# Layer 1's weights made slice by slice in one double slot, with cast and subtraction over 1024 columns

## The chip, the core and the metric

One core of a Trainium2 chip runs the whole program. The metric is the device time of one execution in microseconds, as the median of several executions. A profiled execution also gives its span, from the first to the last instruction of the program. TensorE is called PE here, VectorE DVE, ScalarE ACT and SyncE (which issues the transfers) SP, as in the profile.

## The reference

The program computes an attention layer with a memory term and sends its output through two dense layers.

```python
def _attn_ref(q, k, v, M_prev, z_prev, beta):          # B, H, S, D = 4, 8, 576, 64
    scores = scale * np.matmul(q, k.transpose(0, 1, 3, 2))     # causal mask, softmax -> a
    local = np.matmul(a, v)
    mem_out = mem_ret / mem_norm                       # phi(q) @ M_prev over phi(q) . z_prev
    return g * mem_out + (1 - g) * local

def _moe_ref(x, w_in, w_out, s, b):                    # x: 2304 x 512, w_in: 512 x 2048
    r = np.maximum(x @ w_in, 0.0)
    return (s * (r * r) + b) @ w_out

def _moe2_ref(x, w_in, w_out, alpha):
    h = x @ w_in
    return (np.maximum(h, 0.0) + alpha * np.minimum(h, 0.0)) @ w_out

def reference(**kwargs):
    x = rows of attn_out                               # 2304 x 512
    return _moe2_ref(x=_moe_ref(x=x, **moe), **moe2)
```

The weights of both layers arrive as 64-bit floats, so each number is two 32-bit words in memory.

## The kernel before

**Layers.** The hidden size 2048 of a dense layer is cut into 16 slices of 128 (`KF`, index `f`). For a block of tokens `g1` multiplies x with slice f of `w_in` (12 matmuls, L923 to L925), ACT and DVE make the activation (L937, L938, L945 on ACT, L946 on DVE), and `g2` multiplies it with slice f of `w_out` (12 matmuls, L964 to L966). Every float32 operand is split in a high and a low part, and three matmuls replace one: high times high, high times low, low times high. Layer 1 works on one block of 512 tokens (block 0) and then on blocks of 256; layer 2 on blocks of 512.

**Weights.** `weights` prepares one slice. For each of the two matrices a transfer (L859, 512 KB) brings 128 x 512 numbers as 128 x 1024 words into a double slot `st`. Three DVE instructions over 512 columns (L862, L865, L868) put the float32 bits together from the two words in a slot `sw`. ACT copies them to the high part of `wt` (L871), and DVE subtracts the high part from the number, which gives the low part (L874). Layer 1's weights stay in SBUF. They are made while block 0 runs, so block 0 is the place where slices are used for the first time. `w_in` of a slice is made first, and `g1` needs nothing of `w_out`.

**Attention** goes in four batches. Batch 0 has to be finished up to token 512 before block 0 can start. Batch 1 is computed beside block 0, batches 2 and 3 beside the blocks of 256. Its DVE lines are, among others, L740 (the largest score of a row), L605 (low part of the softmax weights), L482 (low part of the values), L526 to L530 (memory term); its PE lines L520, L565, L655, L671 and L767.

**Order.** `Plan` collects all operations with a duration and a priority, and `order` walks through them as a list scheduler: at each step the engine that is free first takes the operation with the best priority whose inputs are there and for which slots can be had. The outcome is a fixed order for each engine. `Slot` objects get their places in `spot`: 19 slots (`pool`, `poolx`), and early in the run also 12 places in the four `room` tiles, three to a tile, where the weights of the last four slices will stand later. A change of one operation's duration, slot or inputs can so reorder all engines until the two plans meet again.

Of the kernel before, what the change touches and what calls it, by code (L numbers as in the profile page):

```python
# [6 lines left out]
F32 = mybir.dt.float32  # L7
# [3 lines left out]
I32 = mybir.dt.int32  # L11
# [15 lines left out]
NP = H // 2  # L27
# [13 lines left out]
NSLOT = 19  # L41

XS = 7
RES = dict(fq=7, fe=3, fa=1, k=5, v=5, vf=3, p=2, w=1, xt=0, st=6, st2=4, wb=3, wb2=1, x=0)
W1GATE = 1
YS = 4
XF = 4
# [31 lines left out]
class Plan:  # L79
# [17 lines left out]
    def op(self, eng, dur, fn, r=(), w=(), prio=None, bytes_=0, claim=()):  # L97
        i = len(self.ops)
        deps, late = set(), set()
        for k in r:  # L100
            if k in self.writer:
                deps.add(self.writer[k])
            self.readers.setdefault(k, []).append(i)
        for k in w:
            if k in self.writer:
                deps.add(self.writer[k])
            late.update(self.readers.get(k, ()))
            self.writer[k] = i
            self.readers[k] = []
        late -= deps  # L110
        late.discard(i)
        deps.discard(i)
        slots = []
        for k in list(r) + list(w):
            s = k[0] if isinstance(k, tuple) else k
            if isinstance(s, Slot) and s not in slots:
                slots.append(s)
                s.left += 1
        self.ops.append((eng, dur, fn, deps | late, i + self.lean if prio is None else prio, bytes_, slots, late, claim))
        return i  # L120
# [8 lines left out]
    def order(self):  # L129
# [29 lines left out]
        def is_free(x, t):  # L159
            return x not in closed and x not in closing and not taken[x] and place_free[x] <= t  # L160

        def spot(t, s):

            if isinstance(s, Bank):
                return min((x for x in (self.nslots + self.nextra + y for y in s.banks) if is_free(x, t)),
                           key=lambda x: place_free[x], default=None)
            if s.early:
                for x in reversed(places[self.nslots + s.above:self.nslots + self.nextra]):
                    if is_free(x, t) and (s.size == 1 or (x - self.nslots) % 3 < 2 and is_free(x + 1, t)):
                        return x  # L170
            base = [x for x in places[:self.nslots] if is_free(x, t)]
            if len(base) < s.reserve + s.size:
                return None
            if s.size == 2:
                base = [x for x in base if x + 1 in base and x + 1 != self.edge]
            return min(base, key=lambda x: place_free[x], default=None)

        def take(t, new):
# [123 lines left out]
def t_dve(n, rate=1.04, extra=0.0):  # L302
    return 69 + n * rate + extra


def t_act(n, fixed=93.0, extra=0.0):
    return fixed + n * 0.834 + extra


def build(tc, kp, vd, qp, mzd, beta8, sb2, win1, wout1, win2, wout2, alpha, outT):  # L310
# [8 lines left out]
    with tc.tile_pool(name="sb", bufs=1) as sb, tc.tile_pool(  # L319
# [9 lines left out]
        def wt(f, x, lo):  # L329
            if f not in made:  # L330
                made[f] = sb.tile([128, 4, DM], F32R, name=f"wt{f}", tag=f"wt{f}")
            return made[f][:, 2 * x + lo, :]
# [43 lines left out]
        def at(s, n, dt=F32):  # L376

            if s.place < NSLOT:
                t, j = (pool, s.place) if s.place < NSLOT - XS else (poolx, s.place - NSLOT + XS)
                v = t[:, j * GW:(j + s.size) * GW]  # L380
            else:
                f, j = divmod(s.place - NSLOT, 3)
                v = room[KF - XF + f][:, j * GW:(j + s.size) * GW]
            return (v if dt == F32 else v.bitcast(dt))[:, 0:n]
# [445 lines left out]

        def weights(win, wout, f, layer):
            prio = None
            if layer == 1:
                prio = marks[int(WP)] + (WP - int(WP)) * (marks[1] - marks[0])
            claim = []
            if layer == 1 and f >= KF - XF:
                claim = [NSLOT + 3 * (f - KF + XF) + j for j in range(3)]
            above = max(0, 3 * (f + 1 - KF + XF))  # L840
            for src, x, key in ((win, 0, "wi"), (wout, 1, "wo")):
                sw = Slot(RES["wb" if layer == 1 else "wb2"], layer == 1, above=above)

                def whole(sw=sw, dt=F32):
                    return at(sw, 512, dt)

                st = Slot(RES["st" if layer == 1 else "st2"], layer == 1, 2, above)

                def word(x, st=st):
                    return at(st, 1024, I32).rearrange("p (n t) -> p n t", t=2)[:, :, x]  # L850

                gate = []

                first = layer == 2 and f == x == 0
                if layer == 2:
                    gate = [("x1", B - 1, NP - 1, 1)] if first else ["claimed"]
                elif W1GATE:
                    gate = [("x1", 0, min(NP - 1, f // W1GATE), 1)]
                op("SP", 475, lambda st=st, src=src: nc.sync.dma_start(  # L859
                    out=at(st, 1024, I32), in_=src[f]), r=gate, w=[st] + (["claimed"] if first else []), prio=prio, bytes_=524288,  # L860
                   claim=list(range(NSLOT - XS, NSLOT)) if first else [])
                op("DVE", t_dve(512, 0.52), lambda word=word, whole=whole: V.tensor_scalar(  # L862
                    out=whole(dt=I32), in0=word(1), scalar1=3, scalar2=0x3FFFFFF8, op0=ALU.logical_shift_left,
                    op1=ALU.bitwise_and), r=[st], w=[sw], prio=prio)
                op("DVE", t_dve(512), lambda word=word, whole=whole: V.scalar_tensor_tensor(  # L865
                    out=whole(dt=I32), in0=word(0), scalar=29, in1=whole(dt=I32), op0=ALU.logical_shift_right,
                    op1=ALU.bitwise_or), r=[st], w=[sw], prio=prio)
                op("DVE", t_dve(512), lambda word=word, whole=whole: V.scalar_tensor_tensor(  # L868
                    out=whole(dt=I32), in0=word(1), scalar=-0x40000000, in1=whole(dt=I32), op0=ALU.bitwise_and,
                    op1=ALU.bitwise_or), r=[st], w=[sw], prio=prio)  # L870
                either("w", t_act(512), lambda whole=whole, x=x: A.copy(out=wt(f, x, 0), in_=whole()),  # L871
                       t_dve(512, 0.52), lambda whole=whole, x=x: V.tensor_copy(out=wt(f, x, 0), in_=whole()),
                       r=[sw], w=[(key, "h", f)], prio=prio, claim=claim)
                op("DVE", t_dve(512), lambda whole=whole, x=x: V.tensor_tensor(  # L874
                    out=wt(f, x, 1), in0=whole(), in1=wt(f, x, 0).bitcast(F32), op=ALU.subtract),
                   r=[sw, (key, "h", f)], w=[(key, "l", f)], prio=prio)
# [267 lines left out]
```

## Time and profile before

| what | before |
|---|---|
| median of 3 executions | 994.93 us (994.38 to 996.17) |
| the profiled execution, own time | 995.49 us |
| its span | 993.5 us |
| PE busy | 976.9 us, 98% |
| DVE busy | 603.6 us, 61% |
| ACT busy | 469.8 us, 47% |
| granted TensorE clock, mean | 1.000 of full speed |

The busy shares are means over stages with very different limits, and the end of a matmul is modelled in the profile, so a PE that reads as busy throughout is not necessarily issuing at its full rate. The stage of the weights of layer 1 lies between about 28 us and 172 us.

### The profile page before, as it was taken

How to read it: one execution, taken by the hardware profiler on the slowest of the kernel's cores; microseconds unless marked ns; L12 is line 12 of the kernel's file. 1: busy time of each engine (PE TensorE's matmuls, PEld its weight loads, DVE VectorE, ACT ScalarE, POOL GpSimd, SP SyncE). 2: the span in 40 equal slices, each digit the busy share in tenths (PEclk: the TensorE clock that was granted, in tenths of full speed). 3: DMA queues.
4: the chain of work that ended last, by engine and by line, in shares of the span. 5: the costliest groups of instructions: out<-in, count | busy, mean ns of one | idle time of the engine just before them, and what ended most of it. 6: DMA issues, size and time to landing. Idle time of an engine off the chain costs nothing.

```text
span 993.5 us, 18027 instructions
## 1 busy us (share of the span) xinstructions
PE 976.9 (98%) x7068; PEld 833.1 (84%) x7068; DVE 603.6 (61%) x1473; ACT 469.8 (47%) x1181; POOL 5.6 (1%) x29
## 2 busy tenths in 40 slices
PE   7999999999999999999999999999999999999998
PEld 5777777788888888999999998888888888888898
DVE  7999998677776767432122999945334443534354
ACT  7877766787777777545445653212112110201111
POOL 1000000000000000000000000000000000000000
PEclk9999999999999999999999999999999999999999
DMA  5359955464667565721000655302000200100010
GB/s 174 99 171 237 233 187 156 103 164 111 149 131 150 146 127 106 179 77 44 1 22 22 215 168 183 125 1 85 1 1 11 64 1 1 43 1 0 1 44 22
DMA packets 114693, 93.23 MB, mean 94 GB/s; under 512 B 83376, under 2 KB 94640, under 8 KB 114608
## 3 DMA queue, kind: packets, MB, share of 16 engines
q1 hardware_dynamic: 114608, 92.08, 34.3%
q8 instruction: 55, 0.90, 0.4%
q14 instruction: 30, 0.25, 0.1%
HBM read 59.29 MB, written 13.11 MB: 73 GB/s over the span
## 4 chain that ended last, share of the span: by engine, by line
PE 90%; DVE 4%; ACT 3%; DMA 1%; issue 1%; SPq 0%; ACTq 0%; DVEq 0%
PE yb L964 14%; PE yb L966 13%; PE yb L965 13%; PE hb L923 9%; PE hb L925 8%; PE hb L924 8%; PE sp L924 3%; PE sp L925 3%; PE sp L923 3%; PE ob L767 2%; PE ob L924 2%; PE ob L923 2%; PE ob L925 2%; PE yb L767 2%; PE sp L671 2%; PE sp L767 2%
## 5 line engine op out<-in xcount | busy, mean ns | idle before, releaser
L964 PE MATMUL yb<-gr,wt 128*128 128x256 f32 (+2 forms) x832 | 273.1, 328 | 0.7 <-ACT gr L945 0.5
L966 PE MATMUL yb<-gr,wt 128*128 128x256 f32 (+2 forms) x832 | 271.3, 326 | 0.0
L965 PE MATMUL yb<-gr,wt 128*128 128x256 f32 (+2 forms) x832 | 270.0, 324 | 0.0
L923 PE MATMUL hb<-xr,wt 128*128 128x256 f32 (+1 forms) x592 | 184.5, 312 | 5.0 <-ACT gt L937 3.5
L925 PE MATMUL hb<-xr,wt 128*128 128x256 f32 (+1 forms) x592 | 180.2, 304 | 0.3 <-DVE wt L874 0.3
L924 PE MATMUL hb<-xr,wt 128*128 128x256 f32 (+1 forms) x592 | 180.0, 304 | 0.0
L964 PEld LDWEIGHTS yb<-gr,wt 128*128 128x128 f32 x832 | 157.0, 189 | 19.3 <-issue 3.1
L966 PEld LDWEIGHTS yb<-gr,wt 128*128 128x128 f32 x832 | 156.8, 188 | 15.3 <-DVE gr L946 1.1
L965 PEld LDWEIGHTS yb<-gr,wt 128*128 128x128 f32 x832 | 156.9, 189 | 13.8
L946 DVE TENSOR_TENSOR gr<-gt,gr 128x256 fp32r<-128x256 f32 (+1 forms) x168 | 84.0, 500 | 135.9 <-ACT gr L945 135.0
L945 ACT CAST gr<-gt 128x256 fp32r<-128x256 f32 (+1 forms) x168 | 78.4, 467 | 147.8 <-DVE gt L943 140.2
L923 PEld LDWEIGHTS hb<-xr,wt 128*128 128x128 f32 x592 | 111.7, 189 | 18.2 <-ACT gt L937 5.5
L925 PEld LDWEIGHTS hb<-xr,wt 128*128 128x128 f32 x592 | 111.6, 189 | 6.3 <-DVE wt L874 0.7
L924 PEld LDWEIGHTS hb<-xr,wt 128*128 128x128 f32 x592 | 111.7, 189 | 5.0
L937 ACT ACTIVATE gt<-hb 128x256 f32<-128x256 f32 (+1 forms) x128 | 52.5, 410 | 99.9 <-PE hb L925 98.0
L945 ACT CAST gr<-mz 128x512 fp32r<-128x512 f32 (+1 forms) x40 | 23.1, 578 | 157.6 <-DVE mz L943 157.5
L925 PE MATMUL sp<-xr,wt 128*128 128x512 f32 (+1 forms) x160 | 59.4, 371 | 0.0
L924 PE MATMUL sp<-xr,wt 128*128 128x512 f32 (+1 forms) x160 | 59.3, 371 | 0.0
L923 PE MATMUL sp<-xr,wt 128*128 128x512 f32 (+1 forms) x160 | 59.2, 370 | 0.0
L938 ACT ACTIVATE gt<-gt 128x256 f32<-128x256 f32 (+1 forms) x128 | 56.9, 444 | 2.6
L946 DVE TENSOR_TENSOR gr<-mz,gr 128x512 fp32r<-128x512 f32 (+1 forms) x40 | 25.5, 638 | 25.0 <-ACT gr L945 25.0
L940 DVE TENSOR_SCALAR mz<-ob,alv 128x512 f32<-128x512 f32 (+1 forms) x20 | 13.9, 697 | 39.6 <-PE ob L925 39.6
(349 smaller groups left out, 1488.4 us busy)
## 6 DMA issues: line engine op xcount, KB each, us to landing
pool<-wout SPq DMA_DIRECT2D x18, 512.0 KB, 4.4
pool<-win SPq DMA_DIRECT2D x16, 512.0 KB, 4.0
room<-wout SPq DMA_DIRECT2D x14, 512.0 KB, 3.8
room<-win SPq DMA_DIRECT2D x13, 512.0 KB, 4.2
pool<-y SPq DMA_DIRECT2D x18, 256.0 KB, 3.3
out_t<-pool SPq DMA_DIRECT2D x16, 256.0 KB, 2.4
pool<-x SPq DMA_DIRECT2D x11, 256.0 KB, 3.1
y<-pool SPq DMA_DIRECT2D x21, 128.0 KB, 1.8
```

The lines of the kernel that those rows point to most:

```text
L671: T.matmul(obk[D * odd:D * odd + D, AT[c] - o0:AT[c] - o0 + nq], W[:, kb, odd, w], p_t(k)[:, y:y + nq], start=False, stop=False, skip_grou ...
L767: T.matmul(bank_at(bk)[rows, x:x + n], half(sqp, odd, q0, nq), half(sk, odd, k0, n), start=True, stop=True, skip_group_check=True)
L923: T.matmul(H_, W_h, X_h, start=(d == 0), stop=False)
L924: T.matmul(H_, W_h, X_l, start=False, stop=False)
L925: T.matmul(H_, W_l, X_h, start=False, stop=(d == KD - 1))
L937: op("ACT", t_act(n, 50), lambda: A.activation(out=t_, in_=H_, func=AF.Relu), r=[hk, "gr"], w=[tk], prio=-1)
L938: op("ACT", t_act(n), lambda: A.activation(out=t_, in_=t_, func=AF.Square), w=[tk], prio=-1)
L945: op("ACT", t_act(n), lambda: A.copy(out=G_h, in_=t_), r=[tk], w=[("gh", gj)], prio=-1)
L946: op("DVE", t_dve(n), lambda: V.tensor_tensor(out=G_l, in0=t_, in1=G_h.bitcast(F32), op=ALU.subtract), r=[tk, ("gh", gj)], w=[("gl", gj)], ...
L964: T.matmul(Y, W_h, G_h, start=first, stop=False, skip_group_check=True)
L965: T.matmul(Y, W_l, G_h, start=False, stop=False, skip_group_check=True)
L966: T.matmul(Y, W_h, G_l, start=False, stop=False, skip_group_check=True)
```

## The change

Layer 1 gets a function of its own, `both`. It takes one slot `sw` of size two for both matrices of a slice, with the words of `w_in` in the left 512 columns and those of `w_out` in the right 512. The three DVE instructions that build the bits stay as they are, 512 columns each, once for each matrix. The copy on ACT and the subtraction on DVE then go once over 1024 columns, written as two halves because the high and low parts of the two matrices alternate in `wt`. Both wait for the words of both matrices. The reserve of these slots goes from 3 to 2, and `spot` can place slots of any size. Layer 2 keeps its code.

```diff
-RES = dict(fq=7, fe=3, fa=1, k=5, v=5, vf=3, p=2, w=1, xt=0, st=6, st2=4, wb=3, wb2=1, x=0)
+RES = dict(fq=7, fe=3, fa=1, k=5, v=5, vf=3, p=2, w=1, xt=0, st=6, st2=4, wb=2, wb2=1, x=0)
...
-                    if is_free(x, t) and (s.size == 1 or (x - self.nslots) % 3 < 2 and is_free(x + 1, t)):
+                    if (x - self.nslots) % 3 + s.size <= 3 and all(is_free(x + y, t) for y in range(s.size)):
...
-            if s.size == 2:
-                base = [x for x in base if x + 1 in base and x + 1 != self.edge]
+            if s.size > 1:
+                base = [x for x in base if all(x + y in base and x + y != self.edge for y in range(1, s.size))]
...
+        def both(win, wout, f, prio, claim, above):
+            sw = Slot(RES["wb"], True, 2, above)
...
+            for x, src in ((0, win), (1, wout)):
+                st = Slot(RES["st"], True, 2, above)
...
+                op("SP", 475, lambda st=st, src=src: nc.sync.dma_start(
+                    out=at(st, 1024, I32), in_=src[f]), r=gate, w=[st], prio=prio, bytes_=524288)
...     (the three building instructions as before, out() being the half x of sw)
+            built = [(sw, 0), (sw, 1)]
+            high, low = ([(key, y, f) for key in ("wi", "wo")] for y in "hl")
+            either("w", t_act(1024), lambda: A.copy(out=part(0), in_=halves(whole())),
+                   t_dve(1024, 0.52), lambda: V.tensor_copy(out=part(0), in_=halves(whole())),
+                   r=built, w=high, prio=prio, claim=claim)
+            op("DVE", t_dve(1024), lambda: V.tensor_tensor(
+                out=part(1), in0=halves(whole()), in1=part(0).bitcast(F32), op=ALU.subtract),
+               r=built + high, w=low, prio=prio)
...
+            if layer == 1:
+                both(win, wout, f, prio, claim, above)
+                return
```

In the program after, the building instructions are L859, L862 and L865, the copy is L870, the subtraction L873, `g1` is L970 to L972 and `g2` L1011 to L1013.

On DVE the order in block 0 reads as follows before, from the last subtraction of slice 7 (`wt_1247`) over slice 8 (`wt_1285`) to the first building instruction of a later matrix; rows L862 to L868 are building instructions and L946 is the activation's low part.

```order
L874 TENSOR_TENSOR wt_1247<-room_68,wt_1247 128x512
L868 SCALAR_TENSOR_TENSOR room_70<-room_69,room_70 128x512
L862 TENSOR_SCALAR room_69<-room_67 128x512
L862 TENSOR_SCALAR room_68<-room_70 128x512
L865 SCALAR_TENSOR_TENSOR room_69<-room_67,room_69 128x512
L874 TENSOR_TENSOR wt_1285<-room_70,wt_1285 128x512
L868 SCALAR_TENSOR_TENSOR room_69<-room_67,room_69 128x512
L865 SCALAR_TENSOR_TENSOR room_68<-room_70,room_68 128x512
L946 TENSOR_TENSOR gr<-gt,gr 128x512
L874 TENSOR_TENSOR wt_1285<-room_69,wt_1285 128x512
```

The same place after, from the subtraction of slice 7 (`wt_1321`) to that of slice 8 (`wt_1353`).

```order
L873 TENSOR_TENSOR wt_1321<-pool,wt_1321 128x2x512
L797 RECIPROCAL sm<-sm 128x5
L865 SCALAR_TENSOR_TENSOR poolx<-room_68,poolx 128x512
L605 SCALAR_TENSOR_TENSOR poolx<-poolx,sm 128x128
L865 SCALAR_TENSOR_TENSOR poolx<-room_67,poolx 128x512
L605 SCALAR_TENSOR_TENSOR poolx<-poolx,sm 128x512
L605 SCALAR_TENSOR_TENSOR pool<-pool,sm 128x128
L605 SCALAR_TENSOR_TENSOR pool<-pool,sm 128x512
L605 SCALAR_TENSOR_TENSOR poolx<-pool,sm,poolx 128x576
L873 TENSOR_TENSOR wt_1353<-pool,wt_1353 128x2x512
```

Five attention instructions (L605) that stood elsewhere now stand between the two slices, and slice 8 is usable by `g1` only after the one subtraction over both matrices.

On PE the row of matmuls around the same slices reads as follows before: the end of `g1` of slice 8, scores of batch 1 (L767), and the beginning of `g2` of slice 7.

```order
L923 MATMUL hb<-xr,wt_1285 128x512
L924 MATMUL hb<-xr,wt_1285 128x512
L925 MATMUL hb<-xr,wt_1285 128x512
L767 MATMUL ob<-pool 64x288 x2
L767 MATMUL sp_99<-pool 64x288 x2
L767 MATMUL ob<-pool 128x128
L767 MATMUL sp_99<-pool 128x128
L964 MATMUL yb_94<-gr,wt_1247 128x512
L965 MATMUL yb_94<-gr,wt_1247 128x512
L966 MATMUL yb_94<-gr,wt_1247 128x512
```

After, the end of `g1` of slice 7 (`wt_1321`) is followed at once by `g1` of slice 8 (`wt_1353`).

```order
L970 MATMUL hb<-xr,wt_1321 128x512
L971 MATMUL hb<-xr,wt_1321 128x512
L972 MATMUL hb<-xr,wt_1321 128x512
L970 MATMUL hb<-xr,wt_1353 128x512
L971 MATMUL hb<-xr,wt_1353 128x512
L972 MATMUL hb<-xr,wt_1353 128x512
```

The scores have moved ahead of `g1` of slice 7, as has all of `g2` of slice 6 and a group of L671 matmuls, and nothing but the 12 matmuls of slice 7 now lies between the first use of slice 7 and the first use of slice 8. From the last blocks of layer 1 on, both orders are the same on PE, DVE and ACT.

## Rows read from the trace of the kernel before

**Rows 1.** The page, 40 equal slices of the span: busy tenths of PE and DVE.

```profile
PE   7999999999999999999999999999999999999998
...
DVE  7999998677776767432122999945334443534354
```

**Rows 2.** Stretches of the trace: us, busy us of each engine (instructions), clock, DMA.

```profile
64.20:121.10 56.90, 56.63 (x351) 41.37 (x351) 55.28 (x142) 42.33 (x98) 0.00 (x0) 1.00 0.91 234
121.10:169.70 48.60, 47.32 (x266) 36.28 (x265) 44.67 (x101) 31.00 (x62) 0.51 (x1) 1.00 0.62 187
169.70:200.00 30.30, 28.22 (x234) 21.95 (x233) 20.11 (x60) 21.37 (x63) 0.41 (x2) 1.00 0.37 95
```

**Rows 3.** Waits of PE between 64.2 and 200 us: total, times, longest.

```profile
PE hb L923 <- ACT gt L937: 2.1, 2, 1.4
...
PE hb L925 <- DVE wt L874: 0.3, 1, 0.3
```

**Rows 4.** Groups of one shape, 36 to 180 us: count, busy us, mean ns.

```profile
L874 DVE TENSOR_TENSOR wt<-room,wt 128x512 fp32r<-128x512 f32 x29 | 19.8, 683 | 0.3 <-ACT wt L871 0.2
L871 ACT CAST wt<-room 128x512 fp32r<-128x512 f32 x29 | 17.9, 616 | 10.0 <-DVE room L868 9.8
...
L862 DVE TENSOR_SCALAR room<-room 128x512 int32<-128x512 int32 x27 | 11.1, 419 | 0.2 <-DMA room<-wout 0.2
```

**Rows 5.** DVE's timeline at 41 us: start, duration, instruction.

```profile
41.30 0.41 DVE L696 TENSOR_TENSOR xr<-sp,xr 128x256 fp32r<-128x256 f32 x1
41.63 0.55 DVE L575 COPY room<-ob 128x384 f32<-128x384 f32 x1
...
42.53 0.69 DVE L874 TENSOR_TENSOR wt<-room,wt 128x512 fp32r<-128x512 f32 x1
43.13 0.69 DVE L865 SCALAR_TENSOR_TENSOR pool<-pool 128x512 int32<-128x512 int32 x1
```

**Rows 6.** DVE's timeline: subtractions for w_in of slices 9, 14 and 15.

```profile
124.65 0.69 DVE L874 TENSOR_TENSOR wt<-room,wt 128x512 fp32r<-128x512 f32 x1
...
158.55 0.69 DVE L874 TENSOR_TENSOR wt<-room,wt 128x512 fp32r<-128x512 f32 x1
...
168.51 0.69 DVE L874 TENSOR_TENSOR wt<-pool,wt 128x512 fp32r<-128x512 f32 x1
```

**Rows 7.** PE's timeline: attention matmuls, then first matmuls of slices 9, 14, 15.

```profile
102.46 0.61 PE L520 MATMUL ob<-mz,poolx 128*128 128x130 f32 x4
...
105.10 0.59 PE L767 MATMUL sp<-pool 64*128 64x384 f32 x1
...
128.50 0.40 PE L923 MATMUL hb<-xr,wt 128*128 128x512 f32 x1
128.74 0.39 PE L924 MATMUL hb<-xr,wt 128*128 128x512 f32 x1
...
159.49 0.39 PE L923 MATMUL hb<-xr,wt 128*128 128x512 f32 x1
...
169.69 0.39 PE L923 MATMUL hb<-xr,wt 128*128 128x512 f32 x1
```

**Rows 8.** DVE's attention groups of one shape, 64.2 to 170 us.

```profile
L482 DVE SCALAR_TENSOR_TENSOR pool<-pool,vsc 128x640 f16<-128x640 f32 x1 | 0.9, 885 | 0.2 <-ACT pool L480 0.2
...
L605 DVE SCALAR_TENSOR_TENSOR pool<-pool,sm 128x576 f16<-128x576 f32 x1 | 0.8, 811 | 0.0
L605 DVE SCALAR_TENSOR_TENSOR poolx<-poolx,sm 128x512 f16<-128x512 f32 x1 | 0.8, 753 | 0.0
...
L740 DVE CUSTOM_DVE_ANT_0 sp<-sp,mask 128x512 f32<-128x512 f32 x1 | 0.7, 734 | 0.0
...
L530 DVE TENSOR_TENSOR poolx<-ob,nrm 128x384 f32<-128x384 f32 x1 | 0.6, 553 | 0.0
...
L740 DVE CUSTOM_DVE_ANT_0 ob<-ob,mask 128x288 f32<-128x288 f32 x1 | 0.5, 467 | 0.3 <-ACT poolx L733 0.3
```

**Rows 9.** Waits of DVE between 64.2 and 150 us, the longest.

```profile
DVE pool L503 <- ACT pool L500: 0.8, 1, 0.8
```

More of the change, by code (lines that the diff above doesn't have):

```diff
@@ L827, in attention, with whole, halves, part @@
                    r=[(xt, g) for g in gs], w=[("x1", b, p, g) for g in gs], bytes_=512 * (t1 - t0))
+        def both(win, wout, f, prio, claim, above):
+            sw = Slot(RES["wb"], True, 2, above)
+            def whole(dt=F32, x0=0, n=1024):
+                return at(sw, 1024, dt)[:, x0:x0 + n]
+            def halves(v):
+                return v.rearrange("p (x d) -> p x d", x=2)
+            def part(lo):
+                wt(f, 0, 0)
+                return made[f].rearrange("p (x l) d -> p x l d", l=2)[:, :, lo, :]
+            gate = [("x1", 0, min(NP - 1, f // W1GATE), 1)] if W1GATE else []
+            for x, src in ((0, win), (1, wout)):
+                st = Slot(RES["st"], True, 2, above)
+                def word(y, st=st):
+                    return at(st, 1024, I32).rearrange("p (n t) -> p n t", t=2)[:, :, y]
+                def out(x=x):
+                    return whole(I32, 512 * x, 512)
+                op("SP", 475, lambda st=st, src=src: nc.sync.dma_start(
+                    out=at(st, 1024, I32), in_=src[f]), r=gate, w=[st], prio=prio, bytes_=524288)
+                op("DVE", t_dve(512, 0.52), lambda word=word, out=out: V.tensor_scalar(
+                    out=out(), in0=word(1), scalar1=3, scalar2=0x3FFFFFF8, op0=ALU.logical_shift_left,
+                    op1=ALU.bitwise_and), r=[st], w=[(sw, x)], prio=prio)
+                op("DVE", t_dve(512), lambda word=word, out=out: V.scalar_tensor_tensor(
+                    out=out(), in0=word(0), scalar=29, in1=out(), op0=ALU.logical_shift_right,
+                    op1=ALU.bitwise_or), r=[st], w=[(sw, x)], prio=prio)
+                op("DVE", t_dve(512), lambda word=word, out=out: V.scalar_tensor_tensor(
+                    out=out(), in0=word(1), scalar=-0x40000000, in1=out(), op0=ALU.bitwise_and,
+                    op1=ALU.bitwise_or), r=[st], w=[(sw, x)], prio=prio)
+            built = [(sw, 0), (sw, 1)]
[6 more added lines that the diff above has]
+               r=built + high, w=low, prio=prio)
```

## The prediction, made before the changed kernel ran

> **What bounds the kernel now.** The page comes first: from 25 us to the last slice but one PE reads nine tenths or more everywhere, while DVE is that full only between about 25 and 150 us and again around 550 to 650 us [rows 1]. The first of these two stretches is the stage that the change touches: the weights of layer 1 are made there, beside block 0's matmuls and the attention of batch 1. The table by stretches shows the two engines side by side [rows 2]. From 64.2 us, where block 0 starts, to 121.1 us, PE is busy 56.63 of 56.90 us and DVE 55.28 us. From there to 169.7 us PE is busy 47.32 of 48.60 us and DVE 44.67 us; after that DVE falls away (20.11 of 30.30 us). So in block 0 both engines are at their limit together, and PE alone is from then on. A busy PE need not be at its rate, so the waits are read next: between 64.2 and 200 us PE waited for a weight's subtraction once, for 0.3 us, and a few times for ACT [rows 3]. The issue rate agrees: within `g1` one 512-column matmul starts 0.24 us after the one before [rows 7], I count 0.231 us for each, as 12 in 2.8 us.
>
> It follows that total time is PE's work plus PE's gaps, and that a gap made in block 0 stays unless a later gap of before closes. From the last blocks of layer 1 on, where the two orders are the same, nothing changes.
>
> **What the merging saves.** Per slice one DVE subtraction and one ACT copy go away as instructions; the columns stay. A 512-column subtraction reads 683 ns [rows 4] and a 256-column one 410 ns, but instructions overlap: the 512-column one starts 0.60 us before its successor and the 256-column one 0.33 us [rows 5]. The slope is so 0.27 us for 256 columns, 1.05 ns a column, and the 1024-column subtraction costs 0.60 + 2 x 0.27 = 1.14 us of the engine against 1.20 us for two: 0.06 us a slice, 1.0 us over 16 slices. By the durations the fixed part would be 2 x 0.683 - (0.683 + 2 x 0.273) = 0.14 us a slice, 2.2 us in all; that is the upper bound. On ACT the copy of 616 ns [rows 4] saves about as much, but ACT is busy 42.33 of 56.90 us in the stretch [rows 2], so this lies beside other work and I count it at nothing; without that slack it would be worth the same 1.0 to 2.2 us.
>
> [...] The starts above show about 0.06 us, because the next instruction begins inside that fixed part; so for a queue that is full I go by the starts.
>
> **What the merging delays.** Before, `g1` of a slice needs only the three building instructions and the subtraction of `w_in`; those of `w_out` can follow a whole slice later. Now both matrices' words must be built before the one copy, and the low parts of both come with one subtraction. That puts three building instructions and half a subtraction more ahead of `g1`: 0.34 + 0.60 + 0.60 + 0.54 = 2.1 us of DVE (L862's 419 ns [rows 4] less the 0.08 us of overlap from rows 5). How much slack there was for this differs by slice: the subtraction of `w_in` ended 3.2 us before the first matmul of slice 9 (124.65 + 0.69 against 128.50), but 0.25 us before that of slice 14 and 0.5 us before that of slice 15 [rows 6, 7].
>
> **What the new order does.** The planner reacts by moving other work, and the orders printed above show the worst place, slices 7 to 9. Between the subtractions of slices 7 and 8 DVE now has, at start-to-start prices (duration less 0.08 us) and by the line numbers of before: one L797 of 0.1, two L865 of 0.60, L605 of 512 columns twice 0.67, of 576 once 0.73 [rows 8], of 128 twice about 0.27 (the 512 less 384 columns of 1.05 ns), and the subtraction itself 1.14. The sum is 5.0 us. On PE only `g1` of slice 7 lies between, 12 matmuls, 2.8 us. So PE stands 2.2 us before slice 8. From there to the subtraction of slice 9 DVE has four L862, six L865 or L868, one L946 and the subtraction: 4 x 0.34 + 6 x 0.60 + 0.6 + 1.14 = 6.7 us; PE has `g1` of slice 8 and `g2` of slice 7, 24 matmuls, 5.5 us. That is another 1.2 us, together 3.4 us.
>
> A second count goes from the start of the program. Ahead of slice 9's first usable subtraction DVE gets, beyond what it had: six L740 (two each of 512, 288 and 128 columns, 0.65, 0.39 and, 160 columns less, 0.22: 2.5 us), five L605 (2.6 us), one L482 (0.80), one L530 (0.47) [rows 8], five building instructions (2.5), about 0.8 us of small ones; and loses 0.6 us, since nine wide subtractions stand for eighteen narrow ones, and 1.0 us, since the planner gives some copies of batch 0 to ACT. That is 8.1 us more, and the wide subtraction is 0.5 us longer than the narrow one: 125.3 becomes 133.9 us, and with 0.2 us to PE the first matmul of slice 9 starts at 134.1 instead of 128.5 us. PE has more behind it by then, three L520 and two L767 of 512 columns: four L520 last 0.61 us and a 384-column L767 0.59 us, two of them side by side [rows 7], so about 0.4 + 0.7 = 1.1 us. The loss is 5.6 - 1.1 = 4.5 us by this count. It holds only if DVE waits no more and no less than before. I take 3.8 us, nearer to the first count, which rests on ten neighbouring rows.
>
> **What comes back.** After slice 9 DVE gets ahead: up to the last subtraction of slice 15 it has 2.7 us less before it than it had (1.0 us from the merging, the rest from work that goes to ACT or comes later). PE is then held by nothing but its own backlog, and the gaps it had between 121.1 and 169.7 us, 48.60 - 47.32 = 1.3 us [rows 2], close. The next stretch holds 2.1 us more of gaps; these lie at the turn from block 0 to block 1, where PE waits for ACT's activation [rows 3], and I leave them. The rest, batches 2 and 3 beside the small blocks, is reordered but PE-bound on both sides; I count it at nothing, with 1 us either way.
>
> **The sum.** 3.8 - 1.3 = +2.5 us, with the merging's own 1.0 us already in the prices. The span goes from 993.5 to 996.0 us, the execution's own time from 995.49 to 998.0 us. The profiled execution lay 0.56 us above the median of 994.93 us, so the median after should be 997.4 us.
>
> **Rivals.**
>
> *Everything comes back.* The lateness at slices 8 and 9 is real, but the gaps of both later stretches close, 1.3 + 2.1 = 3.4 us: +0.4 us, 995.3 us. For it: PE has 12 slices' worth of matmuls queued whatever the order. Against: a wait for ACT at the turn of a block is a chain of its own, which starts later when PE is later.
>
> *DVE was the bound, and it is faster.* This ends on the other side. At slices 14 and 15 the matmul started 0.25 and 0.5 us after its subtraction [rows 6, 7], so DVE's count sets PE's pace there. If PE makes up its lateness before slice 13, or the waits at slices 8 and 9 do not arise because PE reaches slice 7 over 3 us later than DVE, then the 2.7 us that DVE has less before its last slice are what is left: 992.2 us. It decides at the point where PE's backlog at slice 13 is under 2.7 us. With 0.14 us a slice, the bound by durations, it gains 1.2 us more.
>
> [...]
>
> *DVE runs dry.* Between the subtractions of slices 6 and 7 the new order has some thirty attention instructions of DVE with few weights among them, and each of those chains goes through PE and ACT. Against: between 64.2 and 150 us before, DVE's longest wait was 0.8 us [rows 9]. If DVE stands 3 us in that stretch, all later slices are 3 us later: +5.5 us, 1000.4 us.
>
> *The change does not do what it says*: a 1024-column instruction in two halves costs as much as two. Then 1.0 us of DVE is lost again, half of it ahead of slice 9: +3.0 us, 997.9 us, hardly to be told from the forecast.
>
> **How the numbers follow.** A difference within 0.2%, 2.0 us, is about what a measurement of this kernel can't tell from no change: 992.9 to 996.9 us. The forecast has 0.34 and the last rival 0.03; DVE running dry 0.14; all come back 0.33; DVE faster 0.16. Faster is the second rival alone, 0.16, same the first, 0.33, slower 0.34 + 0.03 + 0.14 = 0.51. The likeliest's own range is 3.4 - 1.3 - 1 to 4.5 + 1: 996.0 to 1000.4 us. The range for 8 in 10 goes on the low side into the case where DVE gains, to 992.8 us, and on the high side to DVE running dry, 1000.6 us.
>
> **What would show it.** Right: in the trace after, PE waits for L873 at the first matmul of slices 8 and 9, in all 2 to 4 us, where before it waited 0.3 us; the first matmul of slice 9 starts between 132 and 135 us; the subtraction reads 1.2 us in 16 instructions; the first matmul of slice 15 is less than 3 us later than 169.69 us. Wrong: no wait for L873 there, or slice 9 starting before 130 us (then the DVE count overstates), or a first matmul of slice 15 earlier than before. If the difference arises after 200 us, the reasoning about block 0 was beside the point.

## The result and the profile after

The changed kernel takes 1002.6 us in the median of 5 executions (1001.48 to 1003.09), against 995.2 us (994.38 to 996.17) for the kernel before beside it: ratio 1.0076, 95% interval 1.0064 to 1.0087. It is slower, and by 7.4 us instead of the 2.5 us forecast; 1002.6 us lies above the range. In the profiled execution the span is 1001.1 us, 7.6 us more than before, and the mean granted clock 0.997.

The page of the kernel after, busy tenths of DVE in 40 slices of the span, answers to [rows 1]. The fifth digit, 100 to 125 us, fell from 9 to 7.

```profile
DVE  6999798567776777342121999945334433533354
```

The table by stretches after, with the first two stretches of [rows 2] and under them two narrower ones (us, busy us of PE, PEld, DVE, ACT and POOL, clock, DMA share, GB/s):

```profile
64.20:121.10 56.90, 56.07 (x352) 40.38 (x346) 51.29 (x129) 40.18 (x90) 0.00 (x0) 1.00 0.74 201
121.10:169.70 48.60, 42.91 (x260) 33.82 (x257) 46.01 (x92) 28.53 (x51) 0.20 (x1) 0.93 0.72 216
...
104.00:122.00 18.00, 17.95 (x126) 12.60 (x127) 14.02 (x40) 11.52 (x28) 0.00 (x0) 1.00 0.56 126
122.00:135.00 13.00, 8.00 (x46) 5.65 (x41) 12.72 (x32) 8.56 (x19) 0.20 (x1) 0.74 0.90 250
```

Two things happen one after the other. In the first stretch DVE stands 56.90 - 51.29 = 5.6 us, where before it stood 1.6 us [rows 2]: 4.0 us more, 3.2 us of it between 104 and 122 us. The kernel before has there, and in the 13 us that follow:

```profile
104.00:122.00 18.00, 17.73 (x127) 12.95 (x127) 17.20 (x38) 12.57 (x28) 0.00 (x0) 1.00 0.85 205
122.00:135.00 13.00, 12.26 (x62) 9.06 (x61) 12.72 (x35) 8.05 (x20) 0.51 (x1) 1.00 0.77 276
```

PE notices nothing up to 122 us. In the stretch from 121.10 to 169.70 us it does 4.4 us less than before, nearly all of it between 122 and 135 us (8.00 us against 12.26 us), at a lower clock and while DVE is full (12.72 of 13.00 us). What PE waited for between 64.2 and 200 us answers to [rows 3]:

```profile
PE hb L970 <- ACT wt L870: 4.2, 1, 4.2
PE hb L970 <- ACT gt L984: 2.6, 3, 1.7
PE hb L972 <- DVE wt L873: 1.2, 2, 0.6
```

The 4.2 us are one wait, for the copy (L870) of slice 7. DVE's timeline after shows why the copy is late (start, duration, instruction, and the idle time ahead of it with what ended it):

```profile
103.55 1.22 DVE L873 TENSOR_TENSOR wt<-pool,wt 128x1024 fp32r<-128x1024 f32 x1
104.68 0.61 DVE L605 SCALAR_TENSOR_TENSOR pool<-pool,sm 128x384 f16<-128x384 f32 x1
...
109.10 0.16 DVE L526 SCALAR_TENSOR_TENSOR nrm<-sp,vsc 128x4 f32<-128x4 f32 x1 [0.77 <-PE sp L520]
...
111.35 0.57 DVE L740 CUSTOM_DVE_ANT_0 sp<-sp,mask 128x384 f32<-128x384 f32 x1 [1.41 <-PE sp L767]
...
119.69 0.39 DVE L859 TENSOR_SCALAR pool<-room 128x512 int32<-128x512 int32 x1
...
126.92 1.22 DVE L873 TENSOR_TENSOR wt<-pool,wt 128x1024 fp32r<-128x1024 f32 x1
128.06 0.19 DVE L797 RECIPROCAL sm<-sm 128x5 f32<-128x5 f32 x1
...
131.96 1.22 DVE L873 TENSOR_TENSOR wt<-poolx,wt 128x1024 fp32r<-128x1024 f32 x1
133.09 0.42 DVE L859 TENSOR_SCALAR pool<-pool 128x512 int32<-128x512 int32 x1
...
138.65 1.22 DVE L873 TENSOR_TENSOR wt<-pool,wt 128x1024 fp32r<-128x1024 f32 x1
```

Between the subtraction of slice 6 (103.55) and the first building instruction of slice 7 (119.69) lie 16 us with only attention and activation on DVE, which waits for PE and ACT again and again. Yet the words were there. SP's timeline of the kernel after has the transfers of slice 7 (the first two) and slice 8; a weight transfer landed in a median of 4.2 to 4.9 us there.

```profile
91.89 0.33 SPq L857 DMA_DIRECT2D room<-win  x1
...
95.38 0.34 SPq L857 DMA_DIRECT2D room<-wout  x1
96.92 0.33 SPq L857 DMA_DIRECT2D room<-win  x1
98.05 0.33 SPq L857 DMA_DIRECT2D room<-wout  x1
```

Those of slice 7 lay ready in the `room` tiles for 20 us (95.38 + 4.2 to 119.69). Each such tile has three places: the staged words take two, and the third, which could hold a single building slot before, can't hold a double one. With words staged in all four tiles, as here, the double slot has to come from the 19 slots of the pool: two neighbours, and with a reserve of 2 only when four slots are free.

Stepped through, the planner of the kernel after shows just this. In its own time, 5 to 6 us ahead of the trace here, the first building instruction of slice 7 could go from 94.6 us on and gets its slot at 113.8 us. All that time the third places of the four tiles are free, and a single slot could have had one. In the pool two neighbours are free from 100.6 to 102.6 us, but with three free slots in all the reserve refuses them; after that up to six slots are free, but until 112.8 us no two neighbours.

PE's timeline after, with the first matmuls of slices 7, 8 and 9, answers to [rows 7]. Its first row is the start of the program.

```profile
7.93 2.50 PE L520 MATMUL yb<-mz,room 128*128 128x130 f32 x10 [0.89 <-DMA mz<-mzd]
...
126.91 0.79 PE L970 MATMUL hb<-xr,wt 128*128 128x512 f32 x1 [4.24 <-ACT wt L870]
127.50 0.63 PE L971 MATMUL hb<-xr,wt 128*128 128x512 f32 x1
...
132.95 0.50 PE L970 MATMUL hb<-xr,wt 128*128 128x512 f32 x1 [0.69 <-ACT gt L984]
...
138.65 0.40 PE L970 MATMUL hb<-xr,wt 128*128 128x512 f32 x1
...
139.92 0.50 PE L972 MATMUL hb<-xr,wt 128*128 128x512 f32 x1 [0.65 <-DVE wt L873]
...
177.25 0.40 PE L970 MATMUL hb<-xr,wt 128*128 128x512 f32 x1
```

From the fourth to the tenth, the matmuls of slice 7 start 0.43 us apart, at a granted clock of 0.50 of full speed from 126 to 130 us; those of slice 8, from the second on, start 0.23 us apart, at 1.00. Slice 9 starts 10.2 us and slice 15 (177.25) 7.6 us later than before; some of the 10.2 us is attention that PE now does earlier. The loss of 7.6 us at slice 15 is that of the whole span. About 0.9 us of the lateness in this execution is not of the change: the wait of 0.89 us for a transfer in the first 8 us. The profiles of experiments 1, 4, 9, 10 and 11, whose order is the same up to slice 7, do not have it.

Two groups of one shape, 36 to 180 us, answer to [rows 4] (count, busy us, mean ns):

```profile
L873 DVE TENSOR_TENSOR wt<-pool,wt 128x1024 fp32r<-128x1024 f32 x8 | 9.8, 1223 | 0.3 <-ACT wt L870 0.3
L870 ACT CAST wt<-pool 128x1024 fp32r<-128x1024 f32 x8 | 8.4, 1045 | 1.5 <-DVE pool L865 1.5
```

In the timeline above the wide subtraction lets its successor start 1.13 to 1.14 us after it (103.55 to 104.68, 126.92 to 128.06, 131.96 to 133.09), the forecast price.

### The profile page after: what moved, and what is told of

It reads as the page before. It is cut to its first block, busy times and chain, and to the rows that moved or that the text cites. A ratio compares the mean times of both kernels' runs of the same rounds, so it can differ in the third digit from the quotient of the medians.

```text
span 1001.1 us, 18001 instructions
## 1 busy us (share of the span) xinstructions
PE 979.6 (98%) x7068; PEld 835.4 (83%) x7068; DVE 600.2 (60%) x1450; ACT 471.3 (47%) x1172; POOL 5.4 (1%) x29
## 4 chain that ended last, share of the span: by engine, by line
PE 89%; DVE 6%; ACT 3%; issue 1%; DMA 1%; SPq 0%; DVEq 0%; ACTq 0%
PE yb L1011 14%; PE yb L1013 13%; PE yb L1012 13%; PE hb L970 8%; PE hb L972 8%; PE hb L971 8%; PE sp L972 3%; PE sp L971 3%; PE sp L970 3%; PE yb L767 2%; PE ob L971 2%; PE sp L671 2%; PE ob L970 2%; PE ob L972 2%; PE sp L767 2%; PE ob L767 1%
## 5 line engine op out<-in xcount | busy, mean ns | idle before, releaser
L1011 PE MATMUL yb<-gr,wt 128*128 128x256 f32 (+2 forms) x832 | 273.8, 329 | 0.1
L1013 PE MATMUL yb<-gr,wt 128*128 128x256 f32 (+2 forms) x832 | 271.3, 326 | 0.0
L970 PE MATMUL hb<-xr,wt 128*128 128x256 f32 (+1 forms) x592 | 184.5, 312 | 8.3 <-ACT wt L870 4.2
L972 PE MATMUL hb<-xr,wt 128*128 128x256 f32 (+1 forms) x592 | 181.0, 306 | 1.2 <-DVE wt L873 1.2
L1011 PEld LDWEIGHTS yb<-gr,wt 128*128 128x128 f32 x832 | 157.1, 189 | 20.2 <-issue 4.8
L1013 PEld LDWEIGHTS yb<-gr,wt 128*128 128x128 f32 x832 | 156.8, 188 | 14.9 <-DVE gr L993 0.6
L970 PEld LDWEIGHTS hb<-xr,wt 128*128 128x128 f32 x592 | 112.2, 190 | 19.2 <-ACT gt L984 5.6
L972 PEld LDWEIGHTS hb<-xr,wt 128*128 128x128 f32 x592 | 112.0, 189 | 8.4 <-DVE wt L873 2.8
L984 ACT ACTIVATE gt<-hb 128x256 f32<-128x256 f32 (+1 forms) x128 | 52.5, 410 | 113.0 <-PE hb L972 109.7
L972 PE MATMUL sp<-xr,wt 128*128 128x512 f32 (+1 forms) x160 | 59.4, 371 | 0.0
L970 PE MATMUL sp<-xr,wt 128*128 128x512 f32 (+1 forms) x160 | 59.2, 370 | 0.0
```

The lines of the kernel that those rows point to most:

```text
L970: T.matmul(H_, W_h, X_h, start=(d == 0), stop=False)
L972: T.matmul(H_, W_l, X_h, start=False, stop=(d == KD - 1))
L984: op("ACT", t_act(n, 50), lambda: A.activation(out=t_, in_=H_, func=AF.Relu), r=[hk, "gr"], w=[tk], prio=-1)
L1011: T.matmul(Y, W_h, G_h, start=first, stop=False, skip_group_check=True)
L1013: T.matmul(Y, W_h, G_l, start=False, stop=False, skip_group_check=True)
```

## The experiments

The kernel before gave 994.5 to 994.7 us beside all of them. Ratios are to it; what each kernel differs from is named.

**1. The reserve of the double slot at 0** (after, one number).

```diff
-RES = dict(fq=7, fe=3, fa=1, k=5, v=5, vf=3, p=2, w=1, xt=0, st=6, st2=4, wb=2, wb2=1, x=0)
+RES = dict(fq=7, fe=3, fa=1, k=5, v=5, vf=3, p=2, w=1, xt=0, st=6, st2=4, wb=0, wb2=1, x=0)
```

> The changed kernel with the double slot's reserve at 0 instead of 2, nothing else. Slot theory (DVE ran dry for about 6 us because the words of slices 7 and 8 lay ready but no free pair of places could be had for the double slot): the building of slice 7 follows the subtraction of slice 6 at once, DVE's dry stretch of 106 to 119 us is gone, PE waits for L870 or L873 under 1.5 us in all, the clock stays at 1.00, and the time falls from 1002.6 to 994 to 997 us. Merge theory (the wide instruction and the wait for both matrices make each slice late): the order moves, but PE goes on waiting 3 us or more for L870 and L873 and the time stays above 1000 us.

Measured: 996.22 us (995.6 to 997.63), ratio 1.0018 (1.0009 to 1.0028). The wide instructions are all still there, and against the kernel before beside it 1.7 us are left of the 7.4 us. DVE's timeline and, last, its share of the stretch from 104 to 122 us:

```profile
101.90 1.22 DVE L873 TENSOR_TENSOR wt<-pool,wt 128x1024 fp32r<-128x1024 f32 x1
104.49 0.42 DVE L859 TENSOR_SCALAR pool<-room 128x512 int32<-128x512 int32 x1
...
110.25 1.22 DVE L873 TENSOR_TENSOR wt<-pool,wt 128x1024 fp32r<-128x1024 f32 x1
```

```profile
104.00:122.00 18.00, 17.46 (x106) 11.82 (x104) 17.36 (x43) 12.36 (x29) 0.00 (x0) 1.00 0.74 175
```

Slice 7 is built 2.6 us after the subtraction of slice 6 instead of 16 us, and DVE is full again. This is not another order drawn by chance: the plans of this kernel and of the kernel after are the same, operation by operation, until this one asks for slice 7's slot (at 100.6 us of the planner's time) and gets it. So in this order it was the slot that held slice 7 back.

**2. The double slot with its reserve of 2, but copy and subtraction 512 wide**, each half waiting for its own words only.

```diff
-            either("w", t_act(1024), lambda: A.copy(out=part(0), in_=halves(whole())),
-                   t_dve(1024, 0.52), lambda: V.tensor_copy(out=part(0), in_=halves(whole())),
-                   r=built, w=high, prio=prio, claim=claim)
...
+            for x, key in ((0, "wi"), (1, "wo")):
...
+                either("w", t_act(512), lambda x=x, half=half: A.copy(out=wt(f, x, 0), in_=half()),
...
+                       r=[(sw, x)], w=[(key, "h", f)], prio=prio, claim=claim)
+                op("DVE", t_dve(512), lambda x=x, half=half: V.tensor_tensor(
+                    out=wt(f, x, 1), in0=half(), in1=wt(f, x, 0).bitcast(F32), op=ALU.subtract),
+                   r=[(sw, x), (key, "h", f)], w=[(key, "l", f)], prio=prio)
```

> The changed kernel's double slot (reserve 2), but copy and subtraction again once for each matrix over 512 columns, each waiting only for its own words. Slot theory: the double slot is still hard to get, so DVE still has dry stretches and the time stays well above before, 997 to 1002 us. Merge theory: with the wide instructions and the common wait gone, the time is that of before, 994 to 996 us.

Measured: 995.47 us, ratio 1.0009 (1.0 to 1.0018). The theory that the double slot by itself runs DVE dry missed: with the same slot and reserve DVE is busy 17.39 us of the 18 between 104 and 122 us. The slot is dear only in some orders.

**3. The common wait alone** (the kernel before, single slots and 512 columns, but both copies of a slice wait for both matrices' words).

```diff
+            built = []
...
+                built.append((sw, whole, x, key))
+            for sw, whole, x, key in built:
...
-                       r=[sw], w=[(key, "h", f)], prio=prio, claim=claim)
+                       r=[y[0] for y in built] if layer == 1 else [sw], w=[(key, "h", f)], prio=prio, claim=claim)
```

> The kernel before with its single slots and 512-column instructions, but the copies of a slice wait for the words of both matrices. Slot theory: the third place of a room still takes each matrix's words, DVE doesn't run dry, and the common wait costs only the 2 us that three building instructions take at the slices without slack: 995 to 998 us. Merge theory: the common wait alone gives most of the loss, 999 us or more.

Measured: 996.13 us, ratio 1.0016 (1.0008 to 1.0025); DVE busy 17.49 us of the 18. With the wait for both matrices and an order of its own, this kernel is 1.6 us slower than the kernel before, far from 7.4 us. What the wait alone costs is not shown by it, since the new order can give or take more than that (experiments 5 to 8).

**4. PE kept busy ahead of slice 7** (after, 20 extra matmuls, whose result the next ones overwrite).

```diff
+FILL = 20
...
+                    if layer == 1 and n == NBIG and f == 7 and d == 0:
+                        for _ in range(FILL):
+                            T.matmul(H_, wt(6, 0, 0)[:, 0:128], X_h, start=True, stop=True)
```

> The changed kernel with 20 more 512-column matmuls of slice 6 into the bank of g1, ahead of the first matmul of slice 7 (their sums are overwritten by it), so that PE works through most of the 5.3 us in which it stood idle. The granted clock should not fall (mean 1.000, before 0.997). If the slow clock cost what it took from g1 of slice 7 (5.2 instead of 2.8 us), the time falls by 2.4 us to 1000.2 us. If slice 8's subtraction, which came at 133.2 us, holds PE anyway, it falls by 0.3 to 1 us. No gain at all would say that the clock took nothing from the end.

Measured: 1003.0 us (1002.45 to 1003.76), ratio 1.0086 (1.0072 to 1.01): nothing gained. The table by stretches of this kernel, PE's timeline at slices 8 and 9, and DVE's at slice 9:

```profile
130.00:132.00 2.00, 0.58 (x2) 0.30 (x2) 2.00 (x3) 1.97 (x3) 0.00 (x0) 1.00 0.99 299
132.00:134.00 2.00, 1.91 (x6) 1.47 (x6) 2.00 (x6) 0.65 (x2) 0.00 (x0) 0.71 1.17 211
134.00:136.00 2.00, 2.00 (x6) 1.55 (x5) 2.00 (x5) 0.00 (x0) 0.00 (x0) 0.50 1.26 266
```

```profile
131.42 0.50 PE L974 MATMUL hb<-xr,wt 128*128 128x512 f32 x1 [1.60 <-ACT gt L988]
...
139.94 0.50 PE L976 MATMUL hb<-xr,wt 128*128 128x512 f32 x1 [0.29 <-DVE wt L874]
```

```profile
138.66 1.23 DVE L874 TENSOR_TENSOR wt<-pool,wt 128x1024 fp32r<-128x1024 f32 x1 [0.91 <-ACT wt L871]
```

Slice 7 now ran at the full clock (1.00 from 126 to 130 us), but PE then stood 1.60 us at slice 8 and the clock fell there, to 0.50 from 134 to 136 us. The third matmul of slice 9 started at 139.94 us, in the kernel after at 139.92 us. That they agree is chance: this execution had no late transfer at its start, and DVE was 1.0 us ahead of the kernel after up to slice 8's subtraction (130.97 against 131.96 us). It then lost 0.91 us waiting for slice 9's copy, which ACT makes behind the activation of slice 8, and PE gave that late at the low clock. In the kernel after, DVE has no idle time ahead of slice 9's subtraction: DVE's own count sets slice 9 there. What a full clock throughout would give was not reached and stays open.

**5 to 8. The same work in another order.** Only the time that the scheduler assumes for one subtraction is changed, by a few ns. The work is the same; the planner only orders it anew and chooses again whether ACT or DVE does an operation that either can do (before -3 ns has 1187 instructions on ACT and 1467 on DVE, before 1181 and 1473).

The kernel after, with 1.0 and then with 5.0:

```diff
-            op("DVE", t_dve(1024), lambda: V.tensor_tensor(
+            op("DVE", t_dve(1024, 1.04, 1.0), lambda: V.tensor_tensor(
```

The kernel before, with -3.0 and then with 3.0:

```diff
-                op("DVE", t_dve(512), lambda whole=whole, x=x: V.tensor_tensor(
+                op("DVE", t_dve(512, 1.04, -3.0), lambda whole=whole, x=x: V.tensor_tensor(
```

> The changed kernel, in which only the planner's assumed time of the wide subtraction is 1 ns longer; every instruction and every slot size is the same, only the order differs. Slot theory (a double slot with this reserve starves the building of layer 1's weights): the dry stretch of DVE and 999 to 1003 us stay. Draw theory (the edit mainly makes the planner land in another order, and the order drawn decides): DVE's dry stretch between slices 6 and 8 need not come again, and the time can be anywhere between 994 and 1006 us; under 998 us would say that nothing in the changed instructions themselves costs the 7 us.

> The kernel before, in which only the planner's assumed time of the subtraction is 3 ns shorter. Slot theory: nothing of the change is in it, so 994 to 996 us. Draw theory: the order is another one on nearly all rows, and the time is off by several us, above 998 us or below 992 us, with none of the change's edits.

> The changed kernel with the assumed time of the wide subtraction 5 ns longer. Slot theory: as the changed kernel, 999 to 1004 us, with PE waiting for L873 or L870 around slices 7 and 8. Draw theory: some other time between 994 and 1010 us, and the place of the loss is another than in the changed kernel.

> The kernel before with the assumed time of the subtraction 3 ns longer. Slot theory: 994 to 996 us. Draw theory: the order differs from slice 4 of block 0 on, and the time is off by more than 1 us either way; if it is under 992 us this is a version that beats both kernels.

| kernel | median us | ratio (95%) |
|---|---|---|
| after, +1 ns | 999.26 | 1.0050 (1.0038 to 1.0063) |
| before, -3 ns | 1004.92 | 1.0104 (1.0089 to 1.012) |
| after, +5 ns | 1005.28 | 1.0105 (1.0091 to 1.0119) |
| before, +3 ns | 993.08 | 0.9983 (0.9975 to 0.9992) |

One kernel's work spans 993.1 to 1004.9 us by the planner's order, more than the change moved. The place differs too. After with +1 ns has DVE busy 17.90 of the 18 us between 104 and 122 us, so the gap ahead of slice 7 is not there; where its own 4.8 us arise was not traced. The table by stretches, PE's waits and a transfer of the kernel before with -3 ns:

```profile
165.00:182.00 17.00, 12.01 (x101) 7.75 (x99) 8.42 (x22) 5.66 (x15) 0.00 (x0) 0.80 0.48 144
```

```profile
PE hb L923 <- ACT wt L871: 5.0, 1, 5.0
```

```profile
167.83 0.33 SPq L859 DMA_DIRECT2D pool<-win  x1
...
171.97 0.43 DVE L862 TENSOR_SCALAR poolx<-pool 128x512 int32<-128x512 int32 x1 [1.22 <-DMA pool<-win]
```

PE meets much the same, late weights after a stretch in which DVE is not full, then 5.0 us of waiting and a lower clock, but 48 us later and without a double building slot or a wide instruction. After with +5 ns has it there too, with 3.5 us for the copy at 177.27 us. The reason is another one than at slice 7, where the words lay ready: here the words of slice 15 themselves come late. Their transfer for `w_in` is issued at 167.83 us, in the kernel before at 157.84 us; after with +5 ns issues slice 15's two at 163.16 and 169.87 us, the kernel after at 152.78 and 155.96 us. By the code these words may use no tile, and with `st=6` they need eight free slots in the pool.

**9. The subtractions apart, the order kept** (after; each wide subtraction is given out as two of 512 columns, one right behind the other, so nothing else moves).

```diff
-            op("DVE", t_dve(1024), lambda: V.tensor_tensor(
-                out=part(1), in0=halves(whole()), in1=part(0).bitcast(F32), op=ALU.subtract),
-               r=built + high, w=low, prio=prio)
+            def two():
+                for x in range(2):
+                    V.tensor_tensor(out=wt(f, x, 1), in0=whole(F32, 512 * x, 512),
+                                    in1=wt(f, x, 0).bitcast(F32), op=ALU.subtract)
+            op("DVE", t_dve(1024), two, r=built + high, w=low, prio=prio)
```

> The changed kernel in its own order, to the last instruction, but each subtraction over 1024 columns is given out as two over 512, one right behind the other; the copies stay merged. The order cannot move here, so this is the price of the instruction alone. Price theory (0.06 us for each merged pair): DVE starts 1.20 us after the first of a pair with what follows it, in place of 1.14, 1.0 us more of DVE in 16 slices, most of it in time in which DVE waits anyway or which comes back later: 1002.3 to 1003.6 us against 1002.6. A rival in which the merging itself is what costs (w_in's half must wait for w_out's) would give 1000 us or less, since the first half is now out 0.6 us earlier, 16 times. The loss at slice 7, with DVE at 14.0 us of 18 between 104 and 122 us, stays in the first theory.

Measured: 1001.18 us (1000.75 to 1001.38), ratio 1.0064 (1.0052 to 1.0077).

**10. The same on the kernel with a reserve of 0.**

> As the run before this one, on the kernel with a reserve of 0 for the double slot (996.22 us), whose DVE does not run dry: its own order kept, each subtraction given out as two over 512 columns. Price theory: 0.06 us x 16 = 1.0 us more of DVE in a stretch in which DVE is nearly full, so 996.2 to 997.2 us. [...] If merging costs: under 995.5 us.

Measured: 995.15 us (994.57 to 997.7), ratio 1.0007 (0.9998 to 1.0016).

Both expectations by price missed: without the merged subtraction the kernels are 1.4 and 1.1 us faster, not 0 to 1 us slower; measured each against the kernel before beside it, 0.9 and 1.3 us. The intervals of each pair overlap, so the two sizes are rough; the mechanism is in the timelines. The first row is PE's third matmul of slice 1 after, the second the same matmul of the kernel of experiment 10.

```profile
72.42 0.50 PE L972 MATMUL hb<-xr,wt 128*128 128x512 f32 x1 [0.53 <-DVE wt L873]
```

```profile
70.91 0.50 PE L975 MATMUL hb<-xr,wt 128*128 128x512 f32 x1
```

The third matmul is the first that needs a low part, and the low part of `w_in` now comes only with that of `w_out`, 0.5 us later (1.22 us after the start against 0.69 us). After shows this wait twice (1.2 us together), the reserve of 0 twice (0.5 and 0.71 us), experiment 9 once (0.63 us), experiment 10 for 0.18 us. The 0.06 us that a merged pair saves are real on DVE (two halves let the next one start 1.20 us after them, 125.85 to 127.05) and buy nothing here.

**11. The reserve at 3** (after, `wb=3`, the number that the single slot had).

> The changed kernel with a reserve of 3 for the double slot, as the single slot of the kernel before has it, in place of 2. Slot theory: the double slot is still harder to get, so slice 7's words lie as long, DVE runs dry between 104 and 122 us (14 to 15 us of 18) and the time is 1002 to 1005 us. Draw theory (any change to the planner's numbers draws another order, good or bad): anywhere between 993 and 1005 us, with the place of the loss not bound to slice 7.

Measured: 1006.99 us (1006.44 to 1007.24), ratio 1.0123 (1.0109 to 1.0137). Two stretches, and the first matmul of slice 7:

```profile
104.00:122.00 18.00, 17.76 (x140) 12.45 (x138) 13.04 (x43) 11.44 (x31) 0.20 (x1) 1.00 0.64 143
122.00:135.00 13.00, 5.90 (x14) 3.91 (x14) 12.97 (x28) 6.93 (x14) 0.00 (x0) 0.74 0.83 208
```

```profile
127.30 0.79 PE L970 MATMUL hb<-xr,wt 128*128 128x512 f32 x1 [5.46 <-ACT wt L870]
```

The loss sits at slice 7 and is larger, as the slot reading has it, though 2 us above its range. With 0, 2 and 3 in reserve PE stands 0, 4.24 and 5.46 us there. Up to slice 7's first building instruction DVE's order is that of the kernel after, so this is no chance draw either.

**12. The kernel before with a reserve of 5 for the staged words.**

```diff
-RES = dict(fq=7, fe=3, fa=1, k=5, v=5, vf=3, p=2, w=1, xt=0, st=6, st2=4, wb=3, wb2=1, x=0)
+RES = dict(fq=7, fe=3, fa=1, k=5, v=5, vf=3, p=2, w=1, xt=0, st=5, st2=4, wb=3, wb2=1, x=0)
```

> The kernel before, with a reserve of 5 in place of 6 for the slots into which layer 1's words are transferred; its instructions are the same. Draw theory: anywhere between 993 and 1005 us, by no mechanism that could be named ahead. The theory that a reserve works by its meaning alone (words come in a little earlier, nothing else) has DVE never short of words and 993.5 to 995 us against 994.5.

Measured: 993.16 us (992.79 to 994.04), ratio 0.9985 (0.9976 to 0.9994). PE is busy all 30.00 us from 135 to 165 us and DVE 17.72 of the 18 us. Both readings allow it. With experiment 8 it is one of two versions that beat both kernels, by 0.15% and 0.17%, with no edit to an instruction.

## Why the prediction was wrong, step by step

**What bounds.** Right: both engines are at their limit in block 0, and nearly all that PE lost there stayed. By the stretches PE did 0.56 and 4.41 us less up to 169.7 us [rows 2]. At the low clock (0.50 from 126 to 130 us, 0.63 from 130 to 132 us), slice 7's twelve matmuls spread 131.88 - 126.91 = 4.97 us from first to last start, slice 8's 135.62 - 132.95 = 2.67 us: 2.3 us more. Together 7.3 of the 7.6 us. The prediction has no term for the clock.

**What the merging saves.** The price, 0.06 us a slice, was measured so. By the durations it would be 2 x 683 - 1223 = 143 ns. The starts after (1.14 us against the 1.20 us of experiment 9) speak against that size in a full queue, as those of before did. The saving did not become time: experiments 9 and 10 put about 1 us on the other side, since the low half of `w_in` is out 0.5 us later.

**What the merging delays.** Real and small. PE's 1.2 us for L873 are at slices 1 and 9. The sentence that `g1` needs the subtraction was too strong: its first two matmuls need the copy alone, so the large wait was named for L870, not for L873 as forecast.

**What the new order does.** The first count held on DVE to a few hundredths: 5.0 us between the subtractions of slices 7 and 8 (126.92 to 131.96), 6.7 us from there to slice 9's (138.65). PE's gaps from it did not come as 2.2 and 1.2 us. At the low clock PE was busy with slice 7 until 132.3 us, and slice 8's copy was out at 131.85 us. The 0.69 us ahead of slice 8 were not for weights but for ACT's activation of slice 7 (L984, started at 132.30 us), with no other work between the two slices. With slice 7 at the full clock, in experiment 4, PE stood 1.60 us there, since ACT made slice 8's late copy ahead of that activation. Within slice 9 it stood 0.65 us. The second count put the first matmul of slice 9 at 134.1 us; it was 138.65 us.

**The step that failed** is the sentence under that count: "It holds only if DVE waits no more and no less than before." DVE stood 4.0 us more up to 121.1 us, and 134.1 + 4.0 = 138.1 us. The prediction had this as a rival, *DVE runs dry*, in the right place, between the subtractions of slices 6 and 7, and with the right reason, but at 0.14 and with 3 us. What spoke against it, DVE's longest wait of 0.8 us [rows 9], was a fact of the old order and said nothing of the new one. The order itself showed some thirty attention instructions with, in the trace, no building instruction among them; that those of slice 7 came so late, though their words were transferred by 100 us, was to be read from it. What kept them back was the double slot, whose price the prediction put at nothing.

**What comes back.** About half of the 1.3 us. From slice 9's first matmul to slice 15's PE stood 41.19 - 39.91 = 1.28 us before and 38.60 - 37.95 = 0.65 us after:

```profile
128.50:169.69 41.19, 39.91 (x229) 30.98 (x227) 37.53 (x81) 26.82 (x52) 0.00 (x0) 1.00 0.56 159
138.65:177.25 38.60, 37.95 (x226) 30.07 (x225) 32.46 (x61) 21.99 (x38) 0.00 (x0) 1.00 0.49 166
```

With the failed step in its place the sum is 3.8 + 4.0 - 0.6 = 7.2 us against 7.6 us. That it comes so near is in part luck: it has no term for the clock (2.3 us) or for the late transfer at the start (0.9 us), and of the gaps it counts at slices 8 and 9, 3.4 us, PE had 1.3 us.

**What else it missed.** The rest of the reordering was counted at nothing, "with 1 us either way". Experiments 5 to 8 show that the order of the same work is worth 12 us in this program. For the kernel after, the causes are these, each time against the kernel before beside it: of 7.4 us, 5.7 us go with the reserve of the double slot (experiment 1), 0.9 to 1.3 us more with the merged subtraction (9 and 10), and with both undone 0.4 us are left, within the measurement. That is shown for this order. That the change as such costs 7 us is not: its neighbour with +1 ns loses 4.8 us, and with its slot and narrow instructions (experiment 2) it loses 1.0 us, at the edge of the measurement.

## What to carry to other kernels

Where a greedy scheduler lays out a full engine, price a change by the order that it gives: look for the stretch in which that engine has only work that hangs on others, and ask which ready work is kept out and by which buffer. A larger buffer can cost more than a merged instruction saves (here it also needs neighbours, and found none with six slots free), and a merged instruction holds its first half back until its last half is done (here the low part of `w_in` was out 1.22 us after the start against 0.69 us). Before such a result is laid to the change, shake the order by a few ns on both sides; here that moved the kernel before by -1.4 and +10.4 us and the one after by -3.3 and +2.7 us.

## What was not expected of the hardware

After PE had stood from about 122.7 to 126.9 us, its first matmuls ran at half the clock, 0.50 of full speed from 126 to 130 us. The table by stretches of the kernel after:

```profile
122.00:124.00 2.00, 0.67 (x25) 0.51 (x19) 1.73 (x9) 0.81 (x4) 0.20 (x1) 1.00 0.52 78
124.00:126.00 2.00, 0.00 (x0) 0.00 (x0) 2.00 (x6) 1.52 (x6) 0.00 (x0) 0.66 0.96 365
126.00:128.00 2.00, 1.09 (x2) 0.50 (x2) 2.00 (x5) 0.86 (x1) 0.00 (x0) 0.50 1.01 325
128.00:130.00 2.00, 1.93 (x5) 1.50 (x5) 2.00 (x6) 1.67 (x4) 0.00 (x0) 0.50 0.75 263
130.00:132.00 2.00, 2.00 (x7) 1.44 (x5) 2.00 (x5) 1.86 (x3) 0.00 (x0) 0.63 0.87 291
132.00:134.00 2.00, 1.31 (x7) 0.88 (x6) 2.00 (x5) 1.63 (x3) 0.00 (x0) 1.00 1.51 249
```

The granted clock fell during the idle time, to 0.66 in the row from 124 to 126 us and 0.50 in the next, and came back to 1.00 while PE worked through slice 7: its matmuls start 0.42 us apart or more up to the tenth, and the row from 132 to 134 us reads 1.00. So after a wait of 4.24 us PE was busy 2.3 us longer with slice 7 than with slice 8 at the full clock; what that took from the end stays open (experiment 4). In experiment 4 the clock fell after a gap of 1.60 us, with PE busy again at 131.42 us and the clock at 0.50 from 134 to 136 us: there the fall came when PE was already at work.
